# Low part of q on GpSimd at all units; the low part of the second layer's output weights by TensorE and ScalarE

## The chip, the cores and the metric

The kernel runs on one core of a Trainium2 chip. The metric is the device time of one execution in microseconds. The kernel before takes 1382.83 us (median of 3 runs, 1382.4 to 1383.42). The engines are named as in the profile: PE is TensorE (PEld its weight loads), DVE is VectorE, ACT is ScalarE, POOL is GpSimd, SP issues most of the DMAs.

## The reference, cut to what matters

Three stages follow each other. The first is attention over 4 batches, 8 heads, 576 positions and 64 dimensions a head, in which each row keeps only its 32 largest scores. The second and third are token-wise layers (2304 tokens, 512 wide, 2048 hidden): the hidden values go through a rational function in the second and through `h * cos(h)` in the third.

```
scores = scale * q @ k^T                    # 576 x 576 for each batch and head
kth    = 32nd largest of each row
attn   = softmax over the scores >= kth
x  = attn @ v                               # as (2304, 512)
h  = x @ w_in;  g = P(h) / (Q(h) + 1e-6);  x = g @ w_out     # layer 1, with a and b
h  = x @ w_in2; g = h * cos(h);            out = g @ w_out2   # layer 2
```

## The kernel before

All large products are made with split operands: a value is rounded to a high part that TensorE takes in one pass, and the low part is the value less its high part. A product is the sum of high x high, high x low and low x high. So each operand costs a rounding (on ACT) and a difference.

The work is cut into 72 units of attention (128 rows of tokens for a pair of heads each) and, for each of 9 blocks k of 256 tokens, 8 groups g of each layer. A unit takes the 32 largest scores by four rounds of MAX8 and three of MATCH_REPLACE8 on DVE, in the tiles `e` (scores) and `hd` (maxima); the exponentials are ACT's (`e<-sS`), the masked product is a SCALAR_TENSOR_TENSOR on DVE. A piece is a fifth of a unit, and `timed` says at which piece each group's step runs (`in1`, `end1`, `out1` of layer 1, `in2`, `mul2`, `out2` of layer 2), so that all three stages run beside each other. The low part of each group's activation, `gg[:, 1]`, is a subtraction on POOL (`low1`, `low2`), and PE waits for it in `out1` (tile `y`) and `out2` (tile `o`).

Two places matter here.

- `split_q` (line 200) rounds a pair of units' q to `qh` on ACT and forms `ql`, the low part, as a 128x512 subtraction. It runs in every second unit, in pieces 3 and 4; PE reads `ql` in `qk` (line 348) of the next unit. For units 20 to 71 (`U0 <= i < U1`) the subtraction stands on DVE, for the others on POOL.
- `conv` (line 267) turns the weights into float32 parts, 128x512 at a time: kinds 0 and 2 are the first weights of the layers, 1 and 3 the second ones, 16 tiles each. DMA brings `raw`; ACT writes `cb`; DVE shifts (TENSOR_SCALAR); POOL adds; ACT rounds to the high part (`w1hi`, `w1o`, `w2hi`, or `ch` for kind 3). Then comes the difference. For kinds 0 and 2 (`CPE`) PE forms it in PSUM with an identity and a negative identity (lines 298 and 299, tile `diff`) and ACT copies it back to `cb` (line 300). For kind 3 (`SUBV`) DVE subtracts (line 303). A DMA takes `cb` to DRAM. For kinds 2 and 3 `cb` and `raw` have 3 buffers each.

The order on each engine is made when the program is built, by a scheduler that knows the program's order. Between pieces 100 and 356 (units 20 to 71) DVE keeps the program's order (`InOrder`), and each POOL instruction waits for the last DVE instruction before it in the program that is neither MAX8 nor MATCH_REPLACE8 (`Behind`), so that POOL's work lies beside DVE's maxima.

Of the kernel before, what the change touches and what calls it, by code (L numbers as in the profile page):

```python
# [10 lines left out]
F32 = mybir.dt.float32  # L11
# [41 lines left out]
WA, PA = 12, 90  # L53
WG, PG = 10, 90
N1, NU, N2, NST, NGG = 2, 2, 3, 4, 3
SUBV = (3,)
CPE = (0, 2)
DGL, E1P, M2P, LAL = 0, 4, (12, 12), 3
DV1, DV2 = 8, 7
KB, VB, XB = 2, 2, 2  # L60
# [70 lines left out]
def body(tc, out, qt, kt, vt, ident_d, w1_d, w1o_d, a_d, b_d, w2_d, w2o_d):  # L131
    nc = tc.nc
    V, A = InOrder(tc, nc.vector, WIN, C0), Windowed(tc, nc.scalar, WA, PA)
    G = Behind(tc, nc.gpsimd, WG, PG, v=V)
    PE, SP = nc.tensor, nc.sync

    with ExitStack() as ctx:
        def pool(name, bufs=1, **k):
            return ctx.enter_context(tc.tile_pool(name=name, bufs=bufs, **k))
# [15 lines left out]
        def open_tmp():  # L155
            es = ExitStack()
            es.tmp = es.enter_context(tc.tile_pool(name="ctmp", bufs=1))
            tmps.append(es)
# [41 lines left out]
        def split_q(i):  # L200
            raw, = qpair[i // 2]
            hi = att.tile([P, 2, BT], F32R, tag="qh", bufs=QHB, name=f"qh{i}")
            lo = att.tile([P, 2, BT], F32R, tag="ql", bufs=QHB, name=f"ql{i}")
            A.activation(hi, raw, AF.Copy)
            qpair[i // 2] = (raw, hi, lo)
            if U0 <= i < U1:
                yield
                V.tensor_sub(lo, raw, hi.bitcast(F32))
            else:
                G.tensor_sub(lo, raw, hi.bitcast(F32))  # L210

        def load_k(i):
            n, pr = units[i]
# [53 lines left out]
        def conv(kind, c, x):  # L267
            nm = f"{kind}_{c}_{x}"
            wd = (w1_d, w1o_d, w2_d, w2o_d)[kind]
            src = wd.bitcast(I32).rearrange("(c p) (f t) -> c p f t", p=P, t=2)[c, :, x * CW:(x + 1) * CW, :]  # L270
            if kind == 2 and len(whi) == 1:
                tmps.pop().close()
                whi.append(pool("wts2").tile([P, NCC, DF], F32R, name="w2hi"))
                open_tmp()
            n1, n2 = (RA, CA) if kind < 2 else (RB, CB)
            raw = tmps[0].tmp.tile([P, CW, 2], I32, tag="raw", bufs=n1, name="raw" + nm)
            SP.dma_start(out=raw, in_=src)
            a = tmps[0].tmp.tile([P, CW], F32, tag="cb", bufs=n2, name="cb" + nm)
            lo, hi, ai = raw[:, :, 0], raw[:, :, 1], a.bitcast(I32)
            A.activation(a, hi.bitcast(F32), AF.Prelu, scale=2.0 ** -112, alpha=-2.0 ** 32)  # L280
            A.activation(lo, lo.bitcast(U32), AF.Copy, scale=2.0 ** -29)

            def rest():
                V.tensor_scalar(ai, ai, 3, 0, op0=ALU.logical_shift_left, op1=ALU.bitwise_or)
                G.tensor_add(ai, ai, lo)
                if kind == 3:
                    h = tmps[0].tmp.tile([P, CW], F32R, tag="ch", bufs=2, name="ch" + nm)
                elif kind == 1:
                    h = w1o[:, c, :]
                else:  # L290
                    h = whi[kind // 2][:, c, x * CW:(x + 1) * CW]
                A.activation(h, a, AF.Copy)
                if kind in CPE:
                    if "d" not in diff:
                        diff["d"] = ps_o.tile([P, 2, 512], F32, tag="o", name="diff")
                    diff["n"] = n = diff.get("n", 0) + 1
                    d = diff["d"][:, n % 2]
                    PE.matmul(d, ident, a, start=True, stop=False)
                    PE.matmul(d, nident, h, start=False, stop=True)
                    A.activation(a, d, AF.Copy)  # L300
                else:
                    if kind in SUBV:
                        V.tensor_sub(a, a, h.bitcast(F32))
                    else:
                        G.tensor_sub(a, a, h.bitcast(F32))
                if kind == 3:
                    SP.dma_start(out=w2o[c, :, 0, :], in_=h.bitcast(F32))
                    SP.dma_start(out=w2o[c, :, 1, :], in_=a)
                elif kind == 1:
                    SP.dma_start(out=w1ol[c], in_=a)  # L310
                else:
                    dst = wlo[kind // 2][4 * x:4 * x + 4, :, c, :].rearrange("g p t -> p g t")
                    SP.dma_start(out=dst, in_=a.rearrange("p (g t) -> p g t", t=P))

            return rest
# [409 lines left out]
        def attention():  # L725
# [5 lines left out]
            for i in range(nu + 1):  # L731
# [11 lines left out]
                for p in range(5):  # L743
# [26 lines left out]
                    if p == SQ and i % 2 == 0 and 8 <= i + 2 < nu:  # L770
                        sq = split_q(i + 2)
                        next(sq, None)
# [73 lines left out]
```

## Time and profile before

| | |
|---|---|
| median of 3 runs | 1382.83 us |
| the profiled execution, its own time | 1386.08 us |
| its span, first to last instruction | 1384.3 us |
| busy, share of the span: PE, DVE, ACT, POOL | 89%, 85%, 78%, 43% |
| mean granted TensorE clock | 0.942 |
| the chain that ended last: PE, DVE, ACT | 41%, 25%, 15% |

The shares are means over stages that differ. Up to about 320 us the weights are converted beside the first 17 units; kind 2 runs from 139 to 241 us, kind 3 from 231 to 320 us. From 345 to 1183 us units 19 to 71 run beside the layers' groups in a pattern that repeats every 8 units, about 126 us. The last 200 us are the last groups of the layers. A granted clock of 1.00 is 2.4 GHz, of 0.50 is 1.2 GHz; a number between is a stretch with some of each. Line 81 is a helper that records most of DVE's, ACT's and POOL's instructions, so they are told apart by their tiles. PE's matmuls overlap in the records, and a float32 one of 512 columns leaves two records.

### The profile page before, as it was taken

To read this page: it belongs to the slowest core of one execution; us is meant where nothing else is said; L and a number is where in the kernel's file an instruction comes from. 1 tells how busy PE (TensorE), PEld (TensorE's weight loads), DVE (VectorE), ACT (ScalarE), POOL (GpSimd) and SP (SyncE) were. 2 spreads that over 40 slices of the span, in tenths; PEclk is the share of its full clock that TensorE was granted. 3 is DMA by queue.
4 is the path that set the end of the run, shared out by engine and by line. 5 is a ranking of instruction groups with operands and counts; after the bars stand their busy time and mean duration, and the time that the engine had idled before them with its cause. 6 is when DMAs were issued, how large, how long until landed. Compare 5 with 4: busy or idle time off the path is not lost.

```text
span 1384.3 us, 24846 instructions
## 1 busy us (share of the span) xinstructions
PE 1233.5 (89%) x8944; PEld 1095.6 (79%) x8944; DVE 1170.6 (85%) x2477; ACT 1080.4 (78%) x1886; POOL 589.7 (43%) x439
## 2 busy tenths in 40 slices
PE   5786776676898999999989999999999999999997
PEld 2444555565798898899889889989899899999986
DVE  6989977999999898998989898989998888666533
ACT  6887778775788787888878888888888788697653
POOL 3676455553356343644553455445453434430000
PEclk9757789777999999999999999999999999999999
DMA  7996668792467666556776665666666678567786
GB/s 238 330 325 214 220 192 250 241 320 94 159 218 228 232 231 204 202 190 222 243 226 226 222 217 191 225 199 208 206 206 238 236 273 283 196 215 251 240 274 217
DMA packets 141547, 314.97 MB, mean 228 GB/s; under 512 B 12016, under 2 KB 28528, under 8 KB 141424
## 3 DMA queue, kind: packets, MB, share of 16 engines
q1 hardware_dynamic: 122832, 261.99, 57.2%
q10 hardware_dynamic: 18592, 51.39, 11.0%
q8 instruction: 71, 1.16, 0.3%
q14 instruction: 52, 0.43, 0.1%
HBM read 278.20 MB, written 35.13 MB: 226 GB/s over the span
## 4 chain that ended last, share of the span: by engine, by line
PE 41%; DVE 25%; ACT 15%; DMA 9%; issue 5%; POOL 5%; ACTq 0%; SPq 0%; POOLq 0%; DVEq 0%
DVE e L81 11%; PE o L636 8%; DVE hd L81 5%; PE h L496 5%; PE h L498 5%; PE h L497 5%; DVE u L81 4%; PE y L567 3%; PE sx L436 3%; PE y L568 3%; PE y L566 2%; DMA raw<-w 2%; POOL gg L81 2%; ACT r L81 2%; ACT L81 2%
## 5 line engine op out<-in xcount | busy, mean ns | idle before, releaser
L81 DVE MAX8 hd<-e 128x8 f32<-128x288 f32 (+1 forms) x576 | 321.0, 596 | 0.0
L81 DVE MATCH_REPLACE8 e<-hd,e 128x288 f32<-128x288 f32 (+1 forms) x432 | 231.0, 541 | 0.0
L636 PE MATMUL o<-w2o,gg 128*128 128x512 f32 x864 | 217.0, 395 | 8.4 <-POOL gg L81 4.2
L636 PEld LDWEIGHTS o<-w2o,gg 128*128 128x128 f32 x864 | 155.2, 188 | 43.0 <-POOL gg L81 8.1
L496 PE MATMUL h<-xh,w1hi 128*128 128x256 f32 x576 | 172.1, 299 | 18.5 <-ACT pt10a L81 3.0
L567 PE MATMUL y<-gg,w1o 128*128 128x256 f32 x576 | 167.4, 291 | 9.2 <-POOL gg L81 9.1
L566 PE MATMUL y<-gg,w1o 128*128 128x256 f32 x576 | 170.7, 296 | 2.9 <-ACT gg L81 2.9
L81 POOL TENSOR_TENSOR gg<-u,gg 128x512 fp32r<-128x512 f32 x64 | 84.9, 1327 | 205.5 <-DVE rr L81 101.5
L568 PE MATMUL y<-gg,w1ol 128*128 128x256 f32 x576 | 166.3, 289 | 2.1 <-DMA w1ol<-w1ol 2.1
L497 PE MATMUL h<-xl,w1hi 128*128 128x256 f32 x576 | 167.1, 290 | 0.0
L498 PE MATMUL h<-xh,lo 128*128 128x256 f32 x576 | 166.7, 289 | 0.0
L498 PE MATMUL h<-x2h,lo 128*128 128x256 f32 x576 | 163.9, 285 | 0.0
L497 PE MATMUL h<-x2l,w2hi 128*128 128x256 f32 x576 | 163.3, 284 | 0.0
L496 PE MATMUL h<-x2h,w2hi 128*128 128x256 f32 x576 | 162.9, 283 | 0.0
L81 POOL TENSOR_TENSOR rr<-rr,hs 128x512 f32<-128x512 f32 x56 | 72.6, 1299 | 163.4 <-DVE rr L81 119.0
L81 DVE TENSOR_TENSOR e<-sS 128x576 f32<-128x576 f32 x144 | 116.5, 849 | 29.1 <-PE sx L423 21.7
L496 PEld LDWEIGHTS h<-xh,w1hi 128*128 128x128 f32 x576 | 114.8, 199 | 24.8 <-ACT pt10a L81 3.2
L81 DVE SCALAR_TENSOR_TENSOR e<-sS,hd,e 128x576 f32<-128x576 f32 x144 | 127.2, 909 | 8.0 <-ACT e L81 7.8
L81 POOL TENSOR_TENSOR cb<-cb,raw 128x512 int32<-128x512 int32 x64 | 93.0, 1456 | 75.2 <-DVE cb L81 68.0
L567 PEld LDWEIGHTS y<-gg,w1o 128*128 128x128 f32 x576 | 113.5, 197 | 11.4 <-POOL gg L81 10.9
L566 PEld LDWEIGHTS y<-gg,w1o 128*128 128x128 f32 x576 | 113.3, 197 | 4.5 <-ACT gg L81 3.4
L568 PEld LDWEIGHTS y<-gg,w1ol 128*128 128x128 f32 x576 | 113.4, 197 | 3.3 <-DMA w1ol<-w1ol 2.5
(1028 smaller groups left out, 3633.1 us busy)
## 6 DMA issues: line engine op xcount, KB each, us to landing
w2o<-w2o SPq DMA_DIRECT2D x144, 512.0 KB, 4.5
lo<-w1lo SPq DMA_DIRECT2D x72, 512.0 KB, 4.1
w1ol<-w1ol SPq DMA_DIRECT2D x72, 512.0 KB, 4.1
lo<-w2lo SPq DMA_DIRECT2D x72, 512.0 KB, 4.7
k<-kdr ACTq DMA_DIRECT2D x44, 576.0 KB, 4.8
raw<-w SPq DMA_DIRECT2D x32, 512.0 KB, 5.5
v<-vt ACTq DMA_DIRECT2D x48, 320.0 KB, 4.7
qr<-qt ACTq DMA_DIRECT2D x36, 256.0 KB, 4.0
```

Of the source, the lines that this page charges most:

```text
L81: r = f(*a, **k)
L436: mm = PE.matmul(o, v[:, kc * P + j * D:kc * P + (j + 1) * D], pj[j][:, kc, qs], start=False, stop=(kc == 3), skip_group_check=True)
L496: PE.matmul(h[:, i, :], wh, xh[:, c, :], start=(c == 0), stop=False)
L497: PE.matmul(h[:, i, :], wh, xl[:, c, :], start=False, stop=False)
L498: PE.matmul(h[:, i, :], lo[:, i, c, :], xh[:, c, :], start=False, stop=(c == NCC - 1))
L566: PE.matmul(y[:, c, :], w1o[:, f, cs], gh[:, i, :], start=(f == 0 and c % 2 == 0), stop=False, skip_group_check=True)
L567: PE.matmul(y[:, c, :], w1o[:, f, cs], gl[:, i, :], start=False, stop=False, skip_group_check=True)
L568: PE.matmul(y[:, c, :], wl[:, i, cs], gh[:, i, :], start=False, stop=(f == NF - 1), skip_group_check=True)
L636: PE.matmul(o[:, t, :], l[:, i, ts], wt[i][:, r], start=(f == 0 and r == 0 and l is gh), stop=(f == NF - 1 and l is gl), skip_group_check= ...
```

## The change

`ql` is subtracted on POOL for all units, so 26 subtractions leave DVE. Kind 3 joins `CPE`, so its 16 differences go through PE and ACT as those of kinds 0 and 2 do, and not through DVE. `SUBV` goes away.

```diff
--- before.py
+++ after.py
@@ -53,8 +53,7 @@
 WA, PA = 12, 90
 WG, PG = 10, 90
 N1, NU, N2, NST, NGG = 2, 2, 3, 4, 3
-SUBV = (3,)
-CPE = (0, 2)
+CPE = (0, 2, 3)
 DGL, E1P, M2P, LAL = 0, 4, (12, 12), 3
 DV1, DV2 = 8, 7
 KB, VB, XB = 2, 2, 2
@@ -205,9 +204,7 @@
             qpair[i // 2] = (raw, hi, lo)
             if U0 <= i < U1:
                 yield
-                V.tensor_sub(lo, raw, hi.bitcast(F32))
-            else:
-                G.tensor_sub(lo, raw, hi.bitcast(F32))
+            G.tensor_sub(lo, raw, hi.bitcast(F32))
 
         def load_k(i):
             n, pr = units[i]
@@ -299,10 +296,7 @@
                     PE.matmul(d, nident, h, start=False, stop=True)
                     A.activation(a, d, AF.Copy)
                 else:
-                    if kind in SUBV:
-                        V.tensor_sub(a, a, h.bitcast(F32))
-                    else:
-                        G.tensor_sub(a, a, h.bitcast(F32))
+                    G.tensor_sub(a, a, h.bitcast(F32))
                 if kind == 3:
                     SP.dma_start(out=w2o[c, :, 0, :], in_=h.bitcast(F32))
                     SP.dma_start(out=w2o[c, :, 1, :], in_=a)
```

In the conversion, DVE's row loses the subtractions (`cb3_5_0` is the sixth tile of kind 3). Before:

```order
L81 TENSOR_SCALAR cb3_6_0_1932<-cb3_6_0_1932 128x512
L81 MATCH_REPLACE e14_2078<-hd_14_2079,e14_2078 128x576 x2
L81 TENSOR_SCALAR cb3_7_0_1987<-cb3_7_0_1987 128x512
L81 TENSOR_TENSOR cb3_5_0_1871<-cb3_5_0_1871,ch3_5_0_1992 128x512
L81 MAX hd_14_2079<-e14_2078 128x8 x2
L81 TENSOR_TENSOR cb3_6_0_1932<-cb3_6_0_1932,ch3_6_0_2042 128x512
L81 MATCH_REPLACE e15_2268<-hd_15_2269,e15_2268 128x288 x2
```

After:

```order
L80 TENSOR_SCALAR cb3_6_0_1940<-cb3_6_0_1940 128x512
L80 MATCH_REPLACE e15_2292<-hd_15_2293,e15_2292 128x288 x2
L80 SCALAR_TENSOR_TENSOR e14_2094,sum1_1008<-sS14_1889,hd_14_2095,e14_2094 128x576
L80 MAX hd_15_2293<-e15_2292 128x8 x2
L80 SCALAR_TENSOR_TENSOR e14_2094,sum1_1008<-sS14_1889,hd_14_2095,e14_2094 128x576
L80 TENSOR_SCALAR cb3_7_0_1997<-cb3_7_0_1997 128x512
```

DVE goes from the shift of one tile to its top-k work, and the rounds of unit 15 stand nearer. ACT's row at the same tiles, before:

```order
L81 ACTIVATE ch3_5_0_1992<-cb3_5_0_1871 128x512
L81 ACTIVATE ch3_6_0_2042<-cb3_6_0_1932 128x512
L81 ACTIVATE raw3_8_0_2035<-raw3_8_0_2035 128x512
L81 ACTIVATE e14_2078<-sS14_1881,nb_14_2080 128x576 x2
L81 ACTIVATE ch3_7_0_2059<-cb3_7_0_1987 128x512
L81 ACTIVATE raw3_9_0_2052<-raw3_9_0_2052 128x512
L81 ACTIVATE cb3_8_0_2037<-raw3_8_0_2035 128x512
```

After:

```order
L80 ACTIVATE ch3_5_0_2002<-cb3_5_0_1877 128x512
L80 ACTIVATE e14_2094<-sS14_1889,nb_14_2096 128x576
L80 ACTIVATE cb3_4_0_1858<-diff_299 128x512
L80 ACTIVATE ch3_6_0_2054<-cb3_6_0_1940 128x512
L80 ACTIVATE raw3_8_0_2047<-raw3_8_0_2047 128x512
L80 ACTIVATE pt14a_2305<-pp14a_2300 128x512
L80 ACTIVATE sS16_2280<-sx_91 128x576
L80 ACTIVATE cb3_5_0_1877<-diff_299 128x512
```

ACT's copies from `diff` stand between the roundings (`ch3_5_0`, `ch3_6_0`) and the attention's work. In the repeating part, POOL's row around unit 50's `ql` (`xs5_2`, `xl5`: attention's output for the next layer; `gg1_4_6`: low part that `out1` waits for), before:

```order
L81 TENSOR_TENSOR q4_6_8568<-q4_6_8568,r4_6_8569 128x512
L81 TENSOR_TENSOR u4_6_8570<-u4_6_8570,w4_6_8567 128x512
L81 TENSOR_TENSOR gg3_3_8738<-rr3_2_8247,gg3_3_8738 128x512
L81 TENSOR_TENSOR xl5_8858<-xs5_0_7298,xh5_8857 128x512
L81 TENSOR_TENSOR xs5_2_8105<-xs5_2_8105,bs5_1_8724 128x512
L81 TENSOR_TENSOR gg1_4_6_8892<-u4_6_8570,gg1_4_6_8892 128x512
L81 TENSOR_TENSOR q4_7_8775<-q4_7_8775,r4_7_8776 128x512
L81 TENSOR_TENSOR u4_7_8777<-u4_7_8777,w4_7_8774 128x512
L81 TENSOR_TENSOR rr3_4_8635<-rr3_4_8635,hs3_4_8636 128x512
L81 TENSOR_TENSOR xl5_8858<-xs5_2_8105,xh5_8857 128x512
```

After:

```order
L80 TENSOR_TENSOR q4_6_8600<-q4_6_8600,r4_6_8601 128x512
L80 TENSOR_TENSOR u4_6_8602<-u4_6_8602,w4_6_8599 128x512
L80 TENSOR_TENSOR gg3_3_8770<-rr3_2_8279,gg3_3_8770 128x512
L80 TENSOR_TENSOR ql50_8847<-qr50_8767,qh50_8846 128x512
L80 TENSOR_TENSOR xl5_8890<-xs5_0_7330,xh5_8889 128x512
L80 TENSOR_TENSOR gg1_4_6_8924<-u4_6_8602,gg1_4_6_8924 128x512
L80 TENSOR_TENSOR q4_7_8807<-q4_7_8807,r4_7_8808 128x512
L80 TENSOR_TENSOR u4_7_8809<-u4_7_8809,w4_7_8806 128x512
L80 TENSOR_TENSOR rr3_4_8667<-rr3_4_8667,hs3_4_8668 128x512
L80 TENSOR_TENSOR xs5_2_8137<-xs5_2_8137,bs5_1_8756 128x512
L80 TENSOR_TENSOR gg3_4_8971<-rr3_4_8667,gg3_4_8971 128x512
```

`ql50` stands behind the last low part of its group of instructions, and `xs5_2` goes from ahead of `gg1_4_6` to the fourth place behind it. PE's row where it takes that `gg1_4_6` (`y4` is its product), before:

```order
L416 MATMUL pp48b_8909<-ident_96,e48_8681 128x128 x4
L566 MATMUL y4_7785<-gg1_4_6_8892,w1o_117 128x256
L346 MATMUL sx_91<-k50_3_8671,qh50_8814 128x288
L348 MATMUL sx_91<-k50_3_8671,ql50_8815 128x288
L346 MATMUL sx_91<-k50_3_8671,qh50_8814 128x288
L348 MATMUL sx_91<-k50_3_8671,ql50_8815 128x288
L496 MATMUL h0_5_0_8950<-xh5_8857,w1hi_114 128x256
L497 MATMUL h0_5_0_8950<-xl5_8858,w1hi_114 128x256
```

After:

```order
L410 MATMUL pp48b_8941<-ident_96,e48_8713 128x128 x4
L560 MATMUL y4_7817<-gg1_4_6_8924,w1o_117 128x256
L561 MATMUL y4_7817<-gg1_4_6_8924,w1o_117 128x256
L562 MATMUL y4_7817<-gg1_4_6_8924,w1ol4_6_8850 128x256
L560 MATMUL y4_7817<-gg1_4_6_8924,w1o_117 128x256
```

PE took four products of scores and the first six of `h0_5_0` between its first use of `gg1_4_6` and the second; now the 24 products of `y4` stand together.

## Rows read from the trace of the kernel before

**Rows 1.** Busy us of each engine by stretches: stretch, its length, busy (instructions), clock.
```profile
core 0: us, PE busy (x) PEld busy (x) DVE busy (x) ACT busy (x) POOL busy (x), PEclk, DMA share, GB/s
139.00:182.20 43.20, 28.72 (x141) 20.56 (x141) 41.99 (x77) 35.14 (x67) 21.69 (x15) 0.76 0.65 208
182.20:240.60 58.40, 44.79 (x284) 34.68 (x284) 44.40 (x97) 42.98 (x85) 26.78 (x20) 0.94 0.75 227
240.60:345.00 104.40, 68.94 (x429) 61.41 (x430) 98.53 (x198) 72.55 (x135) 50.08 (x33) 0.74 0.64 217
345.00:1190.00 845.00, 810.15 (x6445) 753.06 (x6444) 770.74 (x1690) 703.42 (x1225) 388.12 (x294) 0.99 0.66 220
840.00:966.00 126.00, 122.15 (x963) 113.36 (x962) 115.67 (x261) 107.09 (x188) 57.28 (x44) 1.00 0.63 209
1190.00:1384.00 194.00, 183.79 (x1321) 170.14 (x1319) 99.25 (x160) 122.00 (x180) 23.16 (x18) 1.00 0.71 234
```

**Rows 2.** PE's waits from 240.6 to 345 us: waiter, releaser, us, times, longest.
```profile
PE pp16a L416 <- DVE e L81: 5.0, 1, 5.0
...
PE pp14a L416 <- DVE e L81: 3.6, 1, 3.6
...
PE pp15a L416 <- DVE e L81: 2.9, 1, 2.9
```

**Rows 3.** Tile `ch`: count, ns min/median/max, first and last start, form.
```profile
L81 DVE TENSOR_TENSOR cb<-cb,ch x16: 665/684/1362, 243.1 to 319.7; 128x512 f32<-128x512 f32 x16
```

**Rows 4.** Tile `diff` from 139 to 241 us, kind 2: ACT's copy.
```profile
L81 ACT ACTIVATE cb<-diff x16: 569/585/604, 150.0 to 240.9; 128x512 f32<-128x512 f32 x16
```

**Rows 5.** PE in order of time around one difference of kind 2: start, us, instruction.
```profile
200.56 1.02 PE L298 MATMUL diff<-cb,ident 128*128 128x512 f32 x2
201.02 0.79 PE L299 MATMUL diff<-w2hi,nident 128*128 128x512 f32 x1
201.65 0.28 PE L496 MATMUL h<-xh,w1hi 128*128 128x256 f32 x1
```

**Rows 6.** ACT's waits from 139 to 240.6 us.
```profile
ACT cb L81 <- DMA w2lo<-cb: 5.8, 5, 4.3
```

**Rows 7.** PE's waits from 350 to 1180 us.
```profile
PE y L567 <- POOL gg L81: 7.0, 6, 2.7
PE o L636 <- POOL gg L81: 4.2, 10, 0.8
```

**Rows 8.** DVE's waits from 350 to 1180 us.
```profile
DVE ql L81 <- ACT qh L81: 40.5, 13, 8.7
```

**Rows 9.** Tile `ql`: its subtraction on either engine.
```profile
L81 DVE TENSOR_TENSOR ql<-qr,qh x26: 671/688/694, 344.9 to 1142.5; 128x512 fp32r<-128x512 f32 x26
L81 POOL TENSOR_TENSOR ql<-qr,qh x6: 1268/1591/1780, 123.3 to 298.0; 128x512 fp32r<-128x512 f32 x6
```

**Rows 10.** POOL in order of time around one `ql`: idle time before in brackets.
```profile
911.61 1.29 POOL L81 TENSOR_TENSOR gg<-rr,gg 128x512 fp32r<-128x512 f32 x1
922.54 1.29 POOL L81 TENSOR_TENSOR gg<-u,gg 128x512 fp32r<-128x512 f32 x1 [9.64 <-DVE rr L81]
```

**Rows 11.** DVE in order of time at the same place.
```profile
912.36 1.41 DVE L81 MAX8 hd<-e 128x8 f32<-128x576 f32 x2
915.61 0.69 DVE L81 TENSOR_TENSOR ql<-qr,qh 128x512 fp32r<-128x512 f32 x1 [1.84 <-ACT qh L81]
916.22 0.74 DVE L81 SCALAR_TENSOR_TENSOR u<-u,nega,w 128x512 f32<-128x512 f32 x1
```

**Rows 12.** PE's first use of that `ql`.
```profile
922.79 0.30 PE L348 MATMUL sx<-k,ql 128*128 128x288 f32 x1
```

**Rows 13.** All engines in order of time where POOL and DVE meet.
```profile
899.83 1.44 POOL L81 TENSOR_TENSOR gg<-rr,gg 128x512 fp32r<-128x512 f32 x1 [4.23 <-ACT gg L81]
...
900.45 1.44 DVE L81 SCALAR_TENSOR_TENSOR e<-sS,hd,e 128x576 f32<-128x576 f32 x1 [0.33 <-ACT e L81]
...
901.81 0.81 DVE L81 SCALAR_TENSOR_TENSOR e<-sS,hd,e 128x576 f32<-128x576 f32 x1
```

## The prediction

> **What bounds the kernel now.** I read the busy times by stretches first, since the mean shares hide that the stages have different limits [rows 1]. The reader is to see three. From 240.6 to 345 us, where kind 3 of the weights is converted, DVE is busy 98.53 of 104.4 us (94.4%), while PE has 66% and ACT 69.5%. From 345 to 1190 us PE is busy 810.15 of 845 us (95.9%) at a clock of 0.99, and DVE 91%. From 1190 us on PE has 94.7% and nothing that the change touches. Then I read the waits of each stretch. In the conversion PE waits for DVE's finished scores, for 5.0, 3.6 and 2.9 us at a time [rows 2]: there DVE is what the others wait for. In the long stretch PE's idle time is 845 - 810.15 = 34.9 us, of which 7.0 + 4.2 = 11.2 us are waits for POOL's low parts [rows 7]. DVE's own largest wait there is the one for `qh`, 40.5 us in 13 places [rows 8]. But DVE is not the bound in that stretch: its time counts only as far as it reaches PE's 34.9 us.
>
> **Kind 3's differences (240 to 345 us).** DVE loses 16 subtractions of 0.684 us, 10.9 us [rows 3]. ACT gains 16 copies of 0.585 us, 9.4 us [rows 4]. PE gains 16 differences; one takes from 200.56 to 201.65 us at full clock, so 1.09 us each and 17.4 us in all, and about twice that at the lower clock level [rows 5]. PE has 104.4 - 68.9 = 35.5 us of idle time in the stretch, which covers 17.4 us and only just covers the double. If that cover is gone, PE becomes a second full engine.
>
> What the stretch then takes depends on which engine sets it. DVE has 98.53 - 10.94 = 87.6 us left; at its present share of 94.4% that is 92.8 us, a gain of 11.6. ACT has 72.55 + 9.36 = 81.9 us. ACT runs its row in order, and the repeating part shows what share it reaches so: 107.09 of 126 us, 85% [rows 1]. At that share ACT needs 96.4 us, a gain of 8.0. The stretch before, 139 to 240.6 us, converts kind 2 by this path and has ACT at (35.14 + 42.98) of 101.6 us, 76.9% [rows 1]; at that share ACT needs 106.5 us, a loss of 2.1. There ACT also waits for the DMA that must empty one of the 3 `cb` buffers, 5.8 us in 5 places [rows 6], and the change makes a kind 3 buffer live longer by the way through PE and back. What is queued behind such a wait on ACT is the attention's exponentials and copies, and so DVE and PE. So the ends are -11.6 and +2.1. I take -5, near their middle, since the nearest single row, 139 to 182.2 us, has DVE full and ACT at 81.3%, which gives 100.7 us or -3.7, and the later half of kind 2 ran at a higher clock.
>
> **The low part of q (345 to 1190 us).** DVE loses 26 subtractions of 0.688 us, 17.9 us [rows 9], and the 40.5 us of waits for `qh` in front of them [rows 8]: some 58 us of a DVE queue that is in order. POOL gains 26 of 1.268 us, its fastest, 33 us [rows 9]. That is hidden, as the place around one of them shows: POOL ends its group with a low part at 911.61 + 1.29 = 912.9 us and starts the next at 922.54, after 9.64 us idle [rows 10]; `qh` comes just before 915.61, where DVE starts `ql` after 1.84 us of waiting [rows 11]; PE takes `ql` first at 922.79 [rows 12]. On POOL it would run from about 915.6 to 916.9 us, 5.9 us early enough. Nothing else of POOL's is behind it until 922.54. If that cover is gone, the next low part is late by 1.3 us and PE waits for it.
>
> What DVE wins reaches the time only by PE's waits for POOL, whose groups start after DVE. All of the 11.2 us [rows 7] is the far end of the gain. The order also moves `xs` behind `gg1` in five blocks, which brings that low part forward by one POOL instruction, some 1.3 us [rows 10]; but PE now asks for it ten products earlier in its row, so I count that as nothing. The other end is a loss, where POOL and DVE hinder each other: at 899.83 POOL's subtraction runs until 901.27, and DVE's product, begun at 900.45, takes 1.44 us where the next one takes 0.81 [rows 13]. On POOL `ql` will often run beside DVE's products, where it ran in their row before. If each held DVE for the whole of its 1.27 us, DVE would lose 26 x (1.27 - 0.69) = 15.1 us, and if none of it was covered, so would the time. I take -5, a little under half of the 11.2 us, since the 40.5 us of waits are more than twice the worst loss.
>
> The Trainium skill has a rule for this, in "SBUF — State Buffer", section "SBUF: two separate sides": GpSimd and a DVE instruction with two SBUF inputs contend for one shared port pair, which whoever starts first holds for its whole instruction, while the other fully blocks. The trace agrees: DVE's 1.44 us is the rest of POOL's instruction, 0.82 us, and some 0.6 us of its own. By this rule alone the edit would cost up to the 15.1 us above; by the rows of waits it gives some back. That result is the third rival.
>
> **The sum.** -5 - 5 = -10 us. The profiled execution took 1386.08 us, of which 1384.3 are its span; it would take about 1376. It lies 3.25 us over the median of the runs, so I forecast 1382.83 - 10 = 1373 us. Its own range is 1366 to 1380.
>
> **Rivals.**
> 1. The whole gain. DVE stays the bound of the conversion and both parts give their far ends: -11.6 - 11.2 = -22.8, 1360 us. For it: DVE at 94.4% [rows 1], PE waiting for DVE [rows 2], and a clock that was granted at 0.94 while differences ran on PE and at 0.74 after they had ceased [rows 1]; with them back, PE's 68.9 us there shrink. Against it: ACT's 81.9 us leave little room, and in 182.2 to 240.6 us DVE was at 76% on this very path. The Trainium skill says in "TensorE: Matmul & The Clock Gate", part 1, that the throttled state is the default and activity releases it; the two stretches agree with that.
> 2. No change. ACT and the three `cb` buffers take DVE's place in the conversion (+2.1), and in the long stretch PE's order, not DVE, sets the pace, so that only about 2 us of its waits go: 1383 us. For it: kind 2's ACT share of 76.9% and its waits for the DMA [rows 1, 6], and PE at 95.9%. Against it: PE's waits for DVE [rows 2].
> 3. Slower. The mechanism is POOL's `ql` holding DVE in its products in each of the 26 units: +15.1, against -5 from the conversion, so 1393 us. It decides as soon as `ql` starts after DVE's last MAX8 of the unit, as it would at 915.6, where MAX8 ends at 913.8 [rows 11], and DVE's lost time reaches PE in full. For it: 1.44 against 0.81 us [rows 13]. Against it: the 1.84 us wait in front of that very `ql` goes with it [rows 11], and in the 13 other units `ql` came without a wait, so POOL can be done with most of it before DVE's products begin.
>
> **Chances.** The forecast 0.47, rival 1 0.20, rival 2 0.17, rival 3 0.16. A measurement of this kernel can tell about 0.2%, 2.8 us, from no change. Faster by more than that: nearly all of the forecast and rival 1, and a little of the rest, 0.66. Within it: most of rival 2 and the edge of the forecast, 0.17. Slower: rival 3 and the bad end of rival 2, 0.17. The range runs from rival 1's 1360 to 1389 us, between rivals 2 and 3, which leaves out about half of rival 1 and most of rival 3.
>
> **What would show it.** In the profile after, the conversion (240.6 us to the end of unit 18) takes 99 us, not 104; DVE's share there falls to some 88%, ACT's rises to some 82%, and the clock is above 0.74. If ACT's waits for `cb`'s DMA are there in kind 3 with more than 6 us, the buffers took the gain. In the long stretch DVE has no wait for `qh`, POOL's idle time falls by about 33 us, and PE's waits for POOL's low parts fall from 11.2 to about 6 us. The forecast is wrong if PE waits in front of line 348 for `ql`, if DVE's products of 0.74 and 0.81 us become longer in the mean by more than 0.2 us, or if the pattern of 8 units takes more than 126 us.

## The result, and the profile after

The change made the kernel slower: 1390.65 us (1389.13 to 1391.31) against 1383.07 us of the kernel before in the same runs, a ratio of 1.0054 with an interval of 1.0036 to 1.0071. The profiled execution took 1390.05 us, its span is 1387.8 us. I had forecast 1373, range 1360 to 1389.

First the busy times by stretches of the kernel after, with the columns of [rows 1]. In it and in the next listings the lines are those of the changed kernel: the helper of line 81 is line 80, and PE's lines are six lower.

```profile
240.60:345.00 104.40, 78.46 (x447) 59.99 (x448) 83.18 (x171) 78.95 (x148) 46.14 (x33) 0.86 0.68 225
345.00:1190.00 845.00, 805.00 (x6408) 749.50 (x6407) 761.74 (x1662) 705.10 (x1222) 421.75 (x317) 1.00 0.65 219
840.00:966.00 126.00, 120.79 (x957) 112.61 (x956) 113.97 (x253) 107.09 (x186) 62.74 (x48) 1.00 0.62 207
```

The work moved as planned. In the conversion DVE fell from 98.53 to 83.18 us, ACT rose from 72.55 to 78.95, PE from 68.94 to 78.46 at a clock of 0.86 and not 0.74. In the long stretch POOL gained 33.6 us. But PE, the engine that is nearly full there, is idle for 40.0 of the 845 us, where it was idle for 34.9.

That is not yet the loss in time. From the first `e<-sS` of unit 20 to the first of unit 71, which is the same work in both, it is 822.1 us in the kernel after and 821.3 before: PE has 5 us more of idle time in it (37.4 against 32.4), but the execution of the kernel before had a granted clock of 0.50 (1.2 GHz) for 10.2 us of it, the other for 3.4 us. The change reaches unit 20 at 366.1 us, the kernel before at 361.6. Since single executions differ by as much (more below), this pair alone does not tell where the loss is.

Next PE's largest waits from 350 to 1180 us, as in [rows 7].

```profile
PE y L561 <- POOL gg L80: 10.8, 8, 2.2
PE sx L340 <- ACT xs L80: 4.2, 5, 0.8
PE o L630 <- POOL gg L80: 3.0, 6, 0.6
```

And DVE's largest, as in [rows 8]:

```profile
DVE e L80 <- PE sx L417: 63.5, 22, 5.7
```

DVE's wait for `qh` is gone, as forecast. In its place stands one for PE's scores, 63.5 us where it was 12.6: DVE is ahead and waits for PE, so what it won is worth nothing by itself. PE's waits for POOL's low parts are 10.8 + 3.0 = 13.8 us where they were 11.2 and should have become 6, and PE now waits 4.2 us in 5 places for `xs`, which ACT must copy out of PSUM before the scores can be written. In the chain that ended last DVE's share, 25% before, is 9%. It is 11% in the faster run e9 below too, so this share alone does not tell the loss:

```profile
PE 57%; ACT 15%; DMA 10%; DVE 9%; POOL 5%; issue 3%; SPq 0%; ACTq 0%; POOLq 0%; DVEq 0%
```

In the conversion (240.6 to 345 us) DVE now waits for ACT to write `cb`; before, this was 2.7 us in 2 places.

```profile
DVE cb L80 <- ACT cb L80: 20.8, 10, 4.7
```

### The profile page after: what moved, and what is told of

The parts are those of the page before. It is cut to its first block, busy times and chain, and to the rows that moved or that the text cites. A ratio compares the mean times of both kernels' runs of the same rounds, so it can differ in the third digit from the quotient of the medians.

```text
span 1387.8 us, 24947 instructions
## 1 busy us (share of the span) xinstructions
PE 1245.3 (90%) x8992; PEld 1097.9 (79%) x8992; DVE 1155.0 (83%) x2435; ACT 1091.4 (79%) x1902; POOL 619.6 (45%) x465
## 4 chain that ended last, share of the span: by engine, by line
PE 57%; ACT 15%; DMA 10%; DVE 9%; POOL 5%; issue 3%; SPq 0%; ACTq 0%; POOLq 0%; DVEq 0%
PE o L630 12%; PE h L490 8%; PE h L492 7%; PE h L491 7%; DVE e L80 5%; PE y L561 4%; PE y L562 4%; PE y L560 4%; PE sx L430 3%; POOL gg L80 2%; PE sx L340 2%; PE sx L342 2%; DVE hd L80 2%; DMA raw<-w 2%; DMA kraw<-kt 2%
## 5 line engine op out<-in xcount | busy, mean ns | idle before, releaser
L490 PE MATMUL h<-xh,w1hi 128*128 128x256 f32 x576 | 168.5, 293 | 14.7 <-ACT pt10a L80 3.0
L80 POOL TENSOR_TENSOR cb<-cb,raw 128x512 int32<-128x512 int32 x64 | 90.2, 1412 | 87.2 <-DVE cb L80 81.8
L490 PEld LDWEIGHTS h<-xh,w1hi 128*128 128x128 f32 x576 | 112.0, 194 | 21.5 <-ACT pt10a L80 3.2
L80 ACT ACTIVATE sS<-sx 128x576 f32<-128x576 f32 x144 | 92.8, 644 | 33.8 <-PE sx L342 28.7
```

What stands on the lines that cost most here:

```text
L80: r = f(*a, **k)
L490: PE.matmul(h[:, i, :], wh, xh[:, c, :], start=(c == 0), stop=False)
```

## The experiments

All ratios are to the kernel before on the same chip. A change of 0.2% is 2.8 us.

**Each part alone, and each part's work left out.** The first two make one half of the change each; the next two take work away from VectorE and give it to nobody. Theory A held the conversion responsible for the loss, theory B the low part of q on GpSimd, which would hold VectorE in its products.

e1, the low part of q alone:
```diff
             if U0 <= i < U1:
                 yield
-                V.tensor_sub(lo, raw, hi.bitcast(F32))
-            else:
-                G.tensor_sub(lo, raw, hi.bitcast(F32))
+            G.tensor_sub(lo, raw, hi.bitcast(F32))
```


> Only the low part of q goes to GpSimd; kind 3's differences stay on VectorE. Theory A (the conversion part costs the time: by unit 19 the changed kernel was 5.0 us late in the traces, and 2.6 us late at unit 60): this one is within 2 us of the kernel before, 1383 to 1385 us. Theory B (GpSimd's subtraction holds VectorE, rival 3 of the prediction): it has nearly the whole loss, 1388 to 1391 us, and VectorE's products of 0.74 us are longer in the mean.

Measured: ratio 1.0051 (1.0033 to 1.007). This half carries the whole loss.

e2, the conversion alone:
```diff
-SUBV = (3,)
-CPE = (0, 2)
+CPE = (0, 2, 3)
```


> Only kind 3's differences go to TensorE and ScalarE; the low part of q stays on VectorE. Theory A: 1387 to 1390 us, with unit 19 some 5 us later than before, and ScalarE or TensorE, not VectorE, waited for in the conversion. Theory B: 1378 to 1384 us, since VectorE is freed of 10.9 us in a stretch where it was busy 94%.

Measured: 0.9988 (0.9974 to 1.0003), no difference that can be told.

e3, kind 3's difference left out:
```diff
-                    if kind in SUBV:
-                        V.tensor_sub(a, a, h.bitcast(F32))
-                    else:
+                    if kind not in SUBV:
                         G.tensor_sub(a, a, h.bitcast(F32))
```


> Kind 3's difference is left out altogether (its low part is then not the weights' low part), so VectorE is freed of 16 subtractions and nobody takes them. It shows what freeing VectorE is worth at all. If VectorE's time was what set the conversion: 1383 - 11 = 1372 us. If ScalarE's in-order row and TensorE stand close behind it: 1377 to 1381 us. If VectorE never set it: 1382 to 1384 us, and then the loss of e2 is all cost of the new way.

Measured: 0.9915 (0.9885 to 0.9946), some 11.8 us less. So DVE's subtraction did cost that much, by DVE's time or by the time for which it holds the tile's buffer, and what the change gains there something else takes back.

e4, the low part of q left out from unit 20 on, PE's work the same:
```diff
             if U0 <= i < U1:
                 yield
-                V.tensor_sub(lo, raw, hi.bitcast(F32))
             else:
                 G.tensor_sub(lo, raw, hi.bitcast(F32))
...
-                            mm = PE.matmul(o, lo[:, j, qc], k[:, j, hs], start=False, stop=True, skip_group_check=True)
+                            mm = PE.matmul(o, (lo if i < U0 else hi)[:, j, qc], k[:, j, hs], start=False, stop=True, skip_group_check=True)
```


> The low part of q is left out for units 20 to 71 (the second score product takes the high part again), so neither VectorE nor GpSimd has it; TensorE's work is the same. If TensorE sets the pace of units 20 to 71, as its 96% say: 1381 to 1384 us. If VectorE's waits for the rounded q were worth something: 1374 to 1379 us, and the distance of e1 to this run is what GpSimd's work costs.

Measured: 1.0142 (1.012 to 1.0164), 20 us slower, though POOL got nothing and DVE lost 18 us of work. This broke every account that I had: no engine has more to do, and POOL can't hold DVE with a subtraction that isn't there. DVE waited for PE's scores even longer (from 345 to 1190 us; in the kernel after it is 63.5 us there too):

```profile
DVE e L81 <- PE sx L422: 82.1, 27, 4.6
```

What e1 and e4 have in common is that the subtraction has left DVE's row. The program is ordered when it is built, and without it the scheduler gives PE and ACT other rows: against the kernel before, PE's row as built differs at 265 places in e1 and at 328 in e4, but at 34 in e2, all of them up to 350 us.

**The order held fast.** So I took the work and the order apart. The next kernels hold PE's and ACT's instructions in the row of another build, by an edge without a semaphore from each instruction to its successor in that row. The waits that the data need stay. POOL and the DMA queues are not held, so their rows can move along (`seen` are the instructions as the program issues them, `steps` the other build's row):

```diff
+    for s in steps:
+        at += s
+        if last is not None:
+            tc.add_manual_dep(seen[at], seen[last].name, ORDER, reason="kept")
+        last = at
```

The edges by themselves change nothing. The kernel before with its own rows held (e6's file with the rows of e5), and e1 with its own (e5's file with the rows of e6), are built into the same programs on every engine as without the edges, waits included; neither was run.

e5, e1's placement in the order of before:

> Low part of q on GpSimd as in the change (conversion as before), but TensorE's and ScalarE's instructions are held in the order in which the kernel before runs them (every wait that the data needs stays; extra order edges only). Theory C (the loss comes from the other order that the schedule gives TensorE and ScalarE once the subtraction has left VectorE): 1380 to 1385 us, ratio 0.996 to 1.001, TensorE's stalls between 352 and 1200 us back from 52 to about 45 us. Theory D (GpSimd: the subtraction waits for its high part in GpSimd's queue, and products behind it come late): it stays at 1390 to 1394, ratio 1.004 to 1.007. Theory E (VectorE paces, and only the order hid the gain): 1370 to 1378.

Measured: 0.9975 (0.9959 to 0.999). The loss of 0.51% is a gain of 0.25%.

e6, the placement of before in the order of e1:

> The kernel before with its work on its engines unchanged (low part of q on VectorE), but TensorE and ScalarE are held in the order of the run that moved only the low part of q. Theory C: the loss comes without the move, 1390 to 1396 us, ratio 1.004 to 1.009. Theory D: 1381 to 1386, ratio 0.998 to 1.002. Theory E: 1390 or more, since the order alone is the price.

Measured: 1.0187 (1.0166 to 1.0209), beyond what theory C allowed. Not one instruction has changed its engine, and it is 26 us slower. DVE's row is that of before; POOL's, which isn't held, differs at 26 places too.

e7, e4 in the order of before:

> Low part of q left out for units 20 to 71 (TensorE multiplies by the high part twice, its work is the same), TensorE and ScalarE held in the order of before. The same without the held order took 1406.7. Theory C: 1376 to 1385, ratio 0.994 to 1.001, so 20 us and more of that run were order. Theory D: as that run or little below, 1395 to 1407. Theory E: 1366 to 1375, since VectorE is rid of 18 us of work and 40 us of waits at no cost.

Measured: 0.9949 (0.993 to 0.9968), against 1.0142 in its own order: 27 us between two orders of the same instructions.

e9, the whole change, held in the order of e2, which in the long stretch is that of before:

> The whole change (low part of q on GpSimd, second layer's output differences by TensorE and ScalarE), with TensorE's and ScalarE's instructions held in the order that the run with the conversion's part alone has (that order differs from the kernel before only around the conversion). Theory C (order is the loss): the sum of that run (ratio 0.9988) and of the low part of q under the order of before (0.9975): 0.994 to 0.998, 1376 to 1383 us. If order isn't the whole of it: 1.002 to 1.007 as the change itself.

Measured: 0.9974 (0.9957 to 0.999). So the change as such is a gain of 0.26%, and its own order costs 0.8%. PE's waits for POOL's low parts in e9 (its lines are 75 higher than those of the kernel after):

```profile
PE y L636 <- POOL gg L84: 3.9, 2, 2.3
PE o L705 <- POOL gg L84: 3.7, 9, 0.6
```

That is 7.6 us against 13.8 in the kernel after. DVE's wait for PE's scores is 38.2 us, not 63.5. Where one of these waits comes from can be read in the rows by time. In the kernel after, at unit 45, PE (and POOL between its rows):

```profile
794.71 0.36 PE L560 MATMUL y<-gg,w1o 128*128 128x256 f32 x1
...
796.48 0.27 PE L430 MATMUL sx<-pt45a,v 128*64 128x128 f32 x1
...
796.66 1.27 POOL L80 TENSOR_TENSOR gg<-u,gg 128x512 fp32r<-128x512 f32 x1 [4.78 <-DVE rr L80]
...
797.99 0.38 PE L561 MATMUL y<-gg,w1o 128*128 128x256 f32 x1 [1.23 <-POOL gg L80]
```

PE asks for the low part of `gg1_4_4` right behind unit 45's products with v, while POOL, released by DVE's `rr`, has only begun it: 1.23 us idle. In e9 the same place:

```profile
791.53 0.27 PE L505 MATMUL sx<-pt45a,v 128*64 128x128 f32 x1
...
792.14 1.28 POOL L84 TENSOR_TENSOR gg<-u,gg 128x512 fp32r<-128x512 f32 x1 [5.05 <-ACT xs L84]
...
792.71 0.38 PE L415 MATMUL sx<-k,qh 128*128 128x288 f32 x1
...
793.32 0.27 PE L565 MATMUL h<-xh,w1hi 128*128 128x256 f32 x1
...
797.32 0.28 PE L636 MATMUL y<-gg,w1o 128*128 128x256 f32 x1
```

POOL starts 0.6 us after unit 45's last product here too (0.2 us in the kernel after). But scores of unit 48 and the products `h0_4_6` stand in between, and PE needs the low part only at 797.32, 3.9 us after it is done. It is one of five such places, one in each of five blocks; in the kernel after each of them costs PE 1.23 or 1.24 us, 6.2 us in all.

To see the whole, I took for each product of PE the time to the next one, less the median for products of its kind, and summed what is over by more than 0.15 us, from 352 to 1215 us. Beside it stands the time of the same stretch at the lower clock level, and the time from unit 20 to unit 71:

```
run     rows of PE, ACT    ql on      stalls   at 1.2 GHz   units 20-71   ratio
e7      before's           left out   39.8 us    0   us     809.6 us    0.9949
e9      e2's               POOL       42.0       3.4        814.1       0.9974
e5      before's           POOL       42.5       0          813.5       0.9975
f3      own                DVE        44.4       0          815.6       0.9975
before  own                DVE        46.1      10.2        821.3       1
after   own                POOL       52.2       3.4        822.1       1.0054
e1      own                POOL       53.0      17.1        825.5       1.0051
e11     ACT's of before    POOL       53.9      17.1        831.5       1.0105
e4      own                left out   58.3      23.9        836.4       1.0142
g1      e1's, y moved      POOL       58.7      23.9        837.6       1.0135
e10     PE's of before     POOL       64.1      34.1        845.7       1.0205
e6      e1's               DVE        70.4       6.8        841.9       1.0187
```

The stalls follow the ratios but for a place or two (f3, e10, e11 and g1 come below). Their sizes do not: e4 has only 6.1 us more of them than the kernel after, and is 12 us slower by the ratios. Much of the rest is the clock. At 1.2 GHz the products of `h` start every 0.21 us (g1 at 805 us) and not every 0.12 (e9 at 793 us), so nearly half of such time is lost: by this estimate e4 loses some 10 us by its clock, e10 some 15. Single executions differ here as well: before has 10.2 us of it, e2 with the same rows 3.4.

The times from unit 20 to unit 71 separate work from order. In the rows of before (from unit 20 on e2's and e12's are the same) it is 821.3 us in the kernel before and 817.7 in e2 with ql on DVE, 813.5, 814.1 and 815.2 in e5, e9 and e12 with ql on POOL. In the change's own rows it is 822.1: 8 us over e9, of which the five places are 6.2. Behind unit 71 all runs take between 199.6 and 202.7 us. Ahead of unit 20 single executions scatter: the ten kernels whose conversion is that of before, with three buffers, reach it between 361.6 and 367.5 us, the kernel before first of all, and the change's conversion reaches it at 366.1 (after), 366.3 (e2) and 360.8 (e9).

Within one order the account of the prediction holds: with ql on POOL 3.6 us of stalls go, with ql left out 6.3.

**Which engine's row?** e10 holds PE's row alone, e11 ACT's alone; otherwise as e5.

> Low part of q on GpSimd; only TensorE is held in the order of before, ScalarE takes the order that the schedule then gives. Without held orders the ratio was 1.0051, with both held 0.9975. Theory C1 (the loss is in TensorE's order): 0.996 to 0.999. Theory C2 (it is ScalarE's order, which makes TensorE's operands late): 1.003 to 1.01.

> Low part of q on GpSimd; only ScalarE is held in the order of before, TensorE is free. Theory C1: 1.003 to 1.01. Theory C2: 0.996 to 0.999.

Measured: 1.0205 (1.0174 to 1.0235) and 1.0105 (1.0074 to 1.0135). Neither theory: both are worse than no holding at all. In these two runs the row of one engine was of no use without the row of the other that it was made with. In e10 PE waits for ACT's `xs`:

```profile
PE sx L400 <- ACT xs L85: 20.7, 11, 2.4
```

**Is the order of before a lucky one?** f3 keeps every instruction of VectorE and changes only what PE reads, which also gives PE another row (275 places).
```diff
                 yield
                 V.tensor_sub(lo, raw, hi.bitcast(F32))
...
-                            mm = PE.matmul(o, lo[:, j, qc], k[:, j, hs], start=False, stop=True, skip_group_check=True)
+                            mm = PE.matmul(o, (lo if i < U0 else hi)[:, j, qc], k[:, j, hs], start=False, stop=True, skip_group_check=True)
```


> Low part of q computed on VectorE as before, and all of VectorE's instructions as before, but TensorE's product for it reads the high part instead (its work is the same, it no longer waits for the low part; the output differs by that). The schedule gives TensorE and ScalarE another order for this too (275 places on TensorE). If the order that the schedule finds is as good as any other: 1380 to 1386, ratio 0.998 to 1.001, since a wait went and nothing came. If the order of before is a lucky one, near which other orders cost 5 to 25 us whatever sets them off: 1388 to 1408, ratio 1.003 to 1.018.

Measured: 0.9975 (0.996 to 0.9989). So another order need not be worse, and the order of before isn't a single lucky one.

**Can the place be mended by itself?** g1 is e1 with its own rows of PE and ACT held, but for the five places of the kind shown: there PE's 23 products `y<-gg1_k_4` go behind `h0_k_6`, much as in e9.
```diff
-pp46b  sx<-pt45  y4<-gg1_4_4 x23  h0_4_6 x16  sx<-k48 x4  h0_4_6 x8  h1_3_4
+pp46b  sx<-pt45  h0_4_6 x16  sx<-k48 x4  h0_4_6 x8  y4<-gg1_4_4 x23  h1_3_4
```


> The run that moved only the low part of q (ratio 1.0051), with its own order of TensorE and ScalarE held, but for one edit: at five places (blocks 2 to 6) the 23 products y<-gg1_k_4 stand behind the 24 products h0_k_6 and the scores among them, as in the order of before, and no longer ahead of them. In that run's profile TensorE waited 1.40 us for GpSimd's gg1_k_4 at each of the five. If these places are what the order costs and nothing moves in behind them: 5 x 1.4 = 7 us less, 1383 to 1387, ratio 0.999 to 1.001. If the cost is spread over the whole order, or the wait only moves to the scores or to ScalarE's tiles: 1388 to 1394, ratio 1.003 to 1.007.

Measured: 1.0135 (1.0115 to 1.0155), 0.8% worse than e1 and outside both ranges. The waits at `y` went from 9.8 to 3.4 us, and new ones stand at `h0`; five of g1's PE waits at `h`, and what is left at `y`, from 350 to 1215 us:

```profile
PE y L640 <- POOL gg L85: 3.4, 3, 2.2
PE h L569 <- ACT pt38a L85: 3.0, 1, 3.0
PE h L569 <- ACT pt46a L85: 2.9, 1, 2.9
PE h L569 <- ACT pt30a L85: 2.9, 1, 2.9
PE h L569 <- ACT pt62a L85: 2.9, 1, 2.9
PE h L569 <- ACT pt54a L85: 2.9, 1, 2.9
```

The tiles `pp` (transposed scores) and `h` share two PSUM buffers. In e1's row the 23 products of `y` are what lets ACT copy `pp46a` out before `h0_4_6` takes its buffer. Moving them uncovers that wait: five times 2.9 us for five times some 1.2 to 1.4. That is some 8 us of the 12 by which g1 is slower. After four of the five waits (all but the first) the granted clock fell as well. Around unit 46, before and after PE's first product of `h0_4_6` at 804.97 us (stretch, its length, busy of PE, PEld, DVE, ACT, POOL, clock, DMA):

```profile
802.00:805.10 3.10, 0.22 (x3) 0.14 (x2) 3.10 (x13) 3.07 (x5) 3.10 (x3) 1.00 0.88 330
805.30:808.50 3.20, 3.20 (x17) 3.20 (x16) 3.20 (x8) 2.44 (x6) 2.46 (x3) 0.50 0.01 2
```

PE stood nearly idle, and then worked at 1.2 GHz. So a stall can cost more than its own length.

**The conversion: who takes VectorE's gain back?** e8 leaves the difference out and lets ACT copy each tile onto itself; f4 has PE's products and no copy.
```diff
-                        V.tensor_sub(a, a, h.bitcast(F32))
+                        A.activation(a, a, AF.Copy)
```


> Low part of q as before. The difference of the second layer's output weights is left out; ScalarE copies each of its 16 tiles onto itself instead (the copy of the change without TensorE's two products). Left out wholly it took 1374.1 (ratio 0.9915), with the change's products and copy 1384.5 (0.999). If ScalarE's copy gives the gain back: 1382 to 1386. If TensorE's products do: 1373 to 1377. If both do: 1378 to 1381.

```diff
-CPE = (0, 2)
+CPE = (0, 2, 3)
...
-                    A.activation(a, d, AF.Copy)
+                    if kind != 3:
+                        A.activation(a, d, AF.Copy)
```


> Low part of q as before. Of the change's conversion part TensorE's 32 products stay, and ScalarE's 16 copies of the result are left out (the stored tile is the undiminished one). Without both the ratio was 0.9915, with ScalarE's copy alone 0.9973, with both 0.9988. If ScalarE's copy is most of the price: 0.991 to 0.994. If TensorE's products are as dear: 0.995 to 0.998.

Measured: 0.9973 (0.9958 to 0.9989) and 0.9963 (0.9945 to 0.9981), against 0.9915 without either and 0.9988 with both. Each gives back more than half of the gain by itself, so they aren't added up. Either makes the tile live longer, and DVE's wait for ACT's next `cb` from 240.6 to 345 us goes the same way: 15.7 us in e8, 8.3 in f4, 21.2 in e2 with both, and none of note in e3. f1 gives `cb` a fourth buffer in the whole change, held in the order that the conversion's part alone gets with four; g2 gives it to the kernel before.
```diff
-RA, CA, RB, CB = 5, 6, 3, 3
+RA, CA, RB, CB = 5, 6, 3, 4
```


> The whole change with four cb buffers instead of three in the second layer's conversion; TensorE and ScalarE held in the order that the conversion's part alone gets with four buffers (over the long stretch that is the order of before). With three buffers and a held order the ratio was 0.9974. If a late cb buffer (held until TensorE's products, ScalarE's copy and the store are done) is what eats VectorE's gain: 0.988 to 0.993. If ScalarE's own time is: 0.995 to 0.999.

> The kernel before with four cb buffers instead of three in the second layer's conversion, and no part of the change; order as the schedule gives it (over the long stretch that of before). If the fourth buffer helps only once TensorE and ScalarE hold the tile longer: 1381 to 1386, ratio 0.998 to 1.001, and the 0.9911 of the change with four buffers belongs to both together. If it helps by itself: 1373 to 1379, ratio 0.992 to 0.996.

Measured: f1 0.9911 (0.9892 to 0.993), g2 0.9966 (0.9951 to 0.9981). f1 beats both kernels, with 1373.56 us. DVE's wait for `cb` from 240.6 to 345 us, in e9 with three buffers:

```profile
DVE cb L84 <- ACT cb L84: 18.6, 9, 4.9
```

And in f1 with four:

```profile
DVE cb L84 <- ACT cb L84: 2.7, 2, 1.9
```

With three buffers DVE could not use its free time. The fourth is worth 0.34% without the change and 0.63% with it; the intervals are too wide to tell these two apart for sure. g2 fell between its two expectations. Two things f1 leaves open. It has other rows of PE and ACT in the conversion than e9, so the buffer is not its only edit. And the buffers serve kind 2 as well: unit 12 begins at 200.0 us in f1 and 201.0 in g2, where it is 209.2 in e9 and 209.5 before, so a part of the gain comes ahead of kind 3.

Two more ways to share the differences out, both with ql on POOL. e12 puts kind 3's on POOL too, held in the order of before; f2 leaves the even tiles to DVE and sends the odd ones through PE and ACT, held in the order which that split gets by itself.
```diff
-SUBV = (3,)
+SUBV = ()
```


> Both subtractions on GpSimd (low part of q, and the second layer's output differences there too, without TensorE and ScalarE), TensorE and ScalarE held in the order of before. If GpSimd's idle time in the conversion stretch (50 of 104 us busy, 16 more subtractions of about 1.3 us) hides the differences: 1366 to 1374 us, ratio 0.988 to 0.993 (the runs without the differences took 0.9915). If GpSimd becomes late there: 1376 to 1384.

```diff
-                if kind in CPE:
+                if kind in CPE or kind == 3 and c % 2:
```


> Low part of q on GpSimd; of the 16 output difference tiles the odd 8 by TensorE and ScalarE, the even 8 on VectorE; TensorE and ScalarE held in the order that this split gets with the low part of q on VectorE. If ScalarE's time is what eats the gain, half of the tiles leaves it half as full and VectorE half as free: 0.992 to 0.996, a little below the change's 0.9974. If the transition from conversion to the long stretch decides by its order, anything from 0.992 to 1.003.

Measured: 1.0019 (1.0001 to 1.0037) and 1.0018 (1.0003 to 1.0033). e12 is outside both its ranges; f2 misses the first and lies in the second, wide one. In e12 POOL had room, 68.77 of 104.4 us busy, and DVE waited 8.3 us for `cb`, less than half of e9's:

```profile
240.60:345.00 104.40, 64.48 (x401) 56.21 (x399) 89.19 (x165) 69.90 (x131) 68.77 (x49) 0.77 0.69 234
```

Yet unit 20 begins at 372.0 and 371.4 us (its first `e<-sS`), 4 to 10 us later than in the ten kernels named above; from there to unit 71 they take 815.2 and 814.8 us, hardly more than e5. e12 loses this between units 16 and 20, f2 between 12 and 20, where the conversion ends. Why was not tested; the held order isn't made for e12's split, but f2's is that of its own split.

## Why the prediction was wrong

**The step that failed** is one clause in the low part of q: PE "now asks for it ten products earlier in its row, so I count that as nothing". I had the change of PE's order in hand and shown, and priced it at zero. Measured, the order of the change costs 0.8% (1.0054 against 0.9974 of e9, 11 us), more than the two terms of the sum together. I looked at one place, where the low part came forward too; at five places like the one at 797.99 it does not, and PE's waits for POOL are 13.8 us and not 6. Rival 2 did say that PE's order sets the pace there, but as an order that stays what it is.

**DVE's term in the long stretch**, -5 us with ends of -11.2 and +15.1, was about right in the order for which it was worked out: e5 gives -0.25%, 3.5 us, and PE's waits for low parts fall from 11.2 to 7.6 in e9, near the 6 forecast. By the traces too: from unit 20 to unit 71 e5, e9 and e12 take 814.3 us in the mean, before and e2, with the same rows, 819.5. Leaving ql out in that order is worth 7.1 us (e7). The bound was named too: PE at 95.9%, DVE's time counting only through PE's waits. What follows from it I did not draw: where PE is full, its order is the first thing to price.

**Rival 3**, the only one on the side of the result, gave 1393 us, and the time came near it by another way. Its mechanism is there, and it does not reach the time. In the long stretch DVE's product with `hd` goes from 842 ns to 864 in the mean, and all of DVE's work with two inputs in SBUF, counted by the means of each kind, becomes some 8 us longer. But in e9, which is faster, it becomes some 13 us longer than in e2 with the same rows of PE and ACT, near the worst case of 15.1. The product with `hd` from 345 to 1190 us (busy us, mean ns, idle time before it) in the kernel before:

```profile
L81 DVE SCALAR_TENSOR_TENSOR e<-sS,hd,e 128x576 f32<-128x576 f32 x104 | 84.1, 842 | 5.1 <-ACT e L81 5.1
```

In the kernel after:

```profile
L80 DVE SCALAR_TENSOR_TENSOR e<-sS,hd,e 128x576 f32<-128x576 f32 x106 | 88.0, 864 | 5.5 <-ACT e L80 5.5
```

In e2, then in e9:

```profile
L80 DVE SCALAR_TENSOR_TENSOR e<-sS,hd,e 128x576 f32<-128x576 f32 x106 | 85.7, 842 | 7.5 <-ACT e L80 7.4
L84 DVE SCALAR_TENSOR_TENSOR e<-sS,hd,e 128x576 f32<-128x576 f32 x107 | 93.8, 910 | 8.5 <-ACT e L84 8.5
```

DVE has that time: it waits for PE's scores for longer than this in both kernels (63.5 and 38.2 us). And e4 is slower without any ql, which that mechanism can't be. No kind of product became longer by the 0.2 us that I had set as the sign.

**The conversion's term**, -5 us with ends of -11.6 and +2.1, was mis-sized: alone it brought 0.12%, 1.7 us, and not surely that. Its far end is right, as e3 brought 11.8 us. Of what takes the gain back the runs point to rival 2's mechanism, ACT and the three `cb` buffers in DVE's place: with a fourth buffer DVE's wait falls from 18.6 to 2.7 us and the time by 0.63% (e9 and f1, whose rows in the conversion differ too). The mark that I set for it was the wrong one. I looked for ACT waiting for `cb`'s DMA, which it did for 4.2 us, for a store of kind 2; the wait shows on DVE, for ACT's write of the next `cb`, 20.8 us.

**The rest.** No wait for ql at PE's score product (line 348 before), POOL's 33 us and the clock above 0.74 came as said. In the conversion DVE's share is 83.18 of 104.4 us, 80%, and ACT's 76%, both under the forecast 88 and 82: no engine became full, they wait for each other along the tile's path. The conversion did not become shorter: unit 18 ends at 351.9 us, 111 us after 240.6 and not 99. Of the marks for a wrong forecast one came true by the letter: the pattern of eight units takes more than 126 us. From unit 50 to unit 58, by the starts of their first `e<-sS`, it is 968.3 - 841.4 = 126.9 us, where it was 965.8 - 840.0 = 125.8. It tells nothing, as from unit 20 to unit 60 it is 635.1 us against 637.1 before. And one reading behind rival 1 was partial: the clock was 0.94 in the second half of kind 2, but 0.76 in its first half, 139 to 182.2 us, with differences on PE there too.

**What stays open** is why the scheduler finds a worse order when the subtraction leaves VectorE, and a good one in f3, where only PE's read changes. In the profiles the five `y` places are most of the long stretch's loss against e9, but they can't be taken out by themselves (g1). How much POOL's row, which moved along with the held ones, adds to e6's loss was not tested either. For the conversion's term the cause is argued from f1, and not shown.

## What to carry to other kernels

Where a scheduler sets the order and one engine is nearly full (95.9% here), a move of work off another engine can first of all be a change of that engine's order: compare the rows of the full engine and its main supplier, and price the places where an operand is asked for earlier. To tell the two effects apart, build the new placement with the old order held, for both engines together. And when work leaves an engine for a longer path, count the buffers on that path before you count the engine's time.

## What I had not expected

The same instructions on the same engines differ by 1.87% in time by their order alone (before and e6), over three times the loss that was to be explained. With half of an order held (e10, e11) it was slower than with none. And freeing an engine at no cost could make the kernel 20 us slower (e4), where the engine set free only waited: DVE's waits for scores rose to 82.1 us.
